# Moving casts, two weight loads and one set of transposes in the ramp of an attention + SwiGLU kernel

## The chip, the cores and the metric

One Trainium2 core of one chip. The metric is the time of one launch in device microseconds; "before" is the median of seven runs. One of these runs was profiled, and the views below are of that execution.

## The reference, cut to what matters

Sigmoid attention (8 batches, 12 heads, 448 positions, 64 per head), and a gated feed-forward block on its output:

```python
scores = q @ k.T / sqrt(64) - log(448)
x = (sigmoid(scores) @ v)              # (8, 12, 448, 64) -> (3584, 768)
g = x @ w_gate                         # 768 -> 1536
h = g * sigmoid(g) * (x @ w_val)
out = h @ w_out                        # 1536 -> 768
```

Inputs and output are float32 in DRAM.

## The kernel before, in words

**Work and names.** The attention is cut into quads: quad n is four heads of one batch, three quads a batch, 24 in all. A quad has seven chunks (n, c). `qk_tile` (L221) makes the scores of a chunk with four matmuls (L228) and `sig_tile` (L237) takes the sigmoid of 128 x 896 scores on ScalarE (L246; split in two halves at L243 for one chunk of each large visit). `pv(n)` (L249) multiplies the seven sigmoid tiles of a quad with v (28 matmuls, L260), and three VectorE copies (L269, and two at L274) bring the result into `xT`. The feed-forward block has, for each batch b, twelve units `ffn1(b, f)` (L301): six matmuls with a slice of w_gate and six with a slice of w_val (L294), then a sigmoid on ScalarE (L312) and two products on VectorE (L314, L318) into `hT`. The weights are held in four slices of three f each (wg, wv: slice i serves f = 3i to 3i+2), loaded by `w_load` (L128) on GpSimd's queue, which also turns float32 into float16 on the way. The second matrix, w_out, is used in `ffn2` (L476) and `ffn2_group` (L418) for two batches at a time.

**Making q and k ready.** For each quad, q and k are loaded (L167) as float32 into a staging tile `st`, cast to bfloat16 into `c16` (L179; on VectorE for quads 2 and 3, on GpSimd from quad 4 on) and transposed into the tile `T`. Quads 0 to 5 are transposed on TensorE (`trans_pe`, L210: fourteen matmuls with the identity, L198, into a PSUM tile, and two VectorE copies out of it, L204), the later ones by DMA (`trans_dma`, L183, on SyncE's queue). The loads of quads 0 to 3 are issued on SyncE at the start, the later ones on GpSimd, as are v (L172) and the weights. `fetch(n)` loads q, k and v of a quad, `casts(n)` casts q and k on GpSimd, `ready(n)` casts and transposes by DMA.

**What sets the order.** The order is written out by hand: each engine runs its instructions in the order of the program text, and waits at the instruction whose input or buffer isn't ready. Buffers come from pools: four `stg` staging tiles, four `c16`, five `v16`, three `T` of each kind. PSUM is one ring of four tiles of two banks each (`ring`, `Banked`, L78), taken in turn by score chunks, PVs, transposes and ffn1 units; a new user waits until the last user of its tile has been read, bank by bank where both declare their banks. A DMA issue on GpSimd's queue also waits, by its semaphore, for the eighth DMA issued before it on that queue.

**The ramp.** Lines 548 to 658 are the hand-written start: chunks of quads 0, 1 and 2, with the transposes, casts, loads and PVs of quads 0 to 2 between them, and the first three ffn1 units (`early`) begun piecewise. In the text, the casts of quad 3 stand behind those of quad 2 and ahead of pv(0).

**After the ramp.** The loop at L689 goes through the list of ffn1 and ffn2 units; between them it puts visits (`attn_step`, L535) of two to four chunks, at times that a small table of costs sets (FU1, FU2, FU3, `vtime`). The visits begin with (3,0), (3,2), (3,4), (4,0), (4,4), (5,0) and so on. A visit with a finished quad before it also does that quad's PV: (4,0) does pv(3). `plan` (L664) names what is issued after the visit that holds a given chunk: fetches, casts, transposes. `post.append` puts a quad into a list whose `trans_pe` is done right after that visit.

Of the kernel before, what the change touches and what calls it, by code (L numbers as in the profile page):

```python
# [19 lines left out]
def kernel(  # L20
# [107 lines left out]
    def w_load(kind, i):  # L128
        cs = slice(i * FW * 128, (i + 1) * FW * 128)
        if kind == "o":  # L130
            nc.gpsimd.dma_start(out=wo16[i], in_=moe_w_out[cs, :].rearrange("(f p) n -> p f n", p=128))
        else:
            w, dst = (moe_w_gate, wg16[i]) if kind == "g" else (moe_w_val, wv16[i])
            nc.gpsimd.dma_start(out=dst, in_=w[:, cs].rearrange("(j p) n -> p j n", p=128))
# [6 lines left out]
    def src_of(n, which):  # L141
        b, j = divmod(n, NJ)
        return (q, k, v)[which][b, 4 * j:4 * j + 4].rearrange("(h w) (p c) d -> (w p) h (c d)", w=2, c=C)
# [17 lines left out]
    def load(n, which, eng=None):  # L161
        ramp = 2 * n + (1 - which)
        st = (
            stg.tile([128, 2, S], FP32, tag=f"R{ramp}", bufs=1, name=f"st{which}_{n}")
            if ramp < NR else stg.tile([128, 2, S], FP32, tag="stg", name=f"st{which}_{n}")
        )
        (eng or nc.sync).dma_start(out=st, in_=src_of(n, which))  # L167
        qkv_st[(n, which)] = st

    def load_v(n):  # L170
        t = v16p.tile([128, 2, S], FP16, tag="v16", name=f"v16_{n}")
        nc.gpsimd.dma_start(out=t, in_=src_of(n, 2))  # L172
        v16[n] = t

    def cast(n, which, eng):
        st = qkv_st.pop((n, which))
        t = c16.tile([128, C, 2, D], BF16, tag="c16", name=f"c16_{which}_{n}")
        q16[(n, which, 0)] = t
        eng.tensor_copy(  # L179
            out=t.rearrange("p c h d -> p h c d"), in_=st.rearrange("p h (c d) -> p h c d", c=C)  # L180
        )
# [28 lines left out]
    def trans_pe(n):  # L210
        D2 = Banked()
        ds = [qkT.tile([128, C, 128], BF16, tag=f"T{w}", name=f"T{w}_{n}") for w in range(2)]
        for f in [trans_part(D2, w, n, w, 0, C, nc.vector, ds[w]) for w in range(2)]:
            f()
        qT[(n, 0)] = ds[0]
# [332 lines left out]
    V, G = nc.vector, nc.gpsimd  # L548
# [46 lines left out]
    def chunk(n, c):  # L595
        sig_tile(n, c, qk_tile(n, c))
# [8 lines left out]
    load_v(1)  # L605
    w_load("v", 0)
    load_v(2)
    load(4, 0, G)
    load(4, 1, G)
    load_v(3)  # L610
# [2 lines left out]
    trans_pe(1)  # L613
    cast(2, 0, V)
    cast(2, 1, V)
    cast(3, 0, V)
    cast(3, 1, V)
    chunk(0, 6)
    for c in range(3):
        chunk(1, c)  # L620
# [1 line left out]
    chunk(1, 3)  # L622
    chunk(1, 4)
    trans_pe(2)
    w_load("g", 1)
    w_load("v", 1)
    load(5, 0, G)
    load(5, 1, G)
    load_v(4)
# [26 lines left out]
    for f, Df in enumerate(early):  # L656
# [5 lines left out]

    post = []
    plan = {  # L664
        (3, 2): ((post.append, 4),),
        (3, 4): ((casts, 5),),
        (4, 0): ((fetch, 6), (post.append, 5)),
        (4, 4): ((ready, 6),),
        (5, 4): ((fetch, 7), (w_out, 0)),
        (6, 0): ((ready, 7), (w_out, 1)),  # L670
# [70 lines left out]
```

## Time and profile before

| | before |
|---|---|
| median of seven runs | 420.0 us (419.19 to 422.33) |
| the profiled execution | 420.84 us |
| its span, first to last instruction | 419.1 us |
| mean granted TensorE clock | 0.996 |
| TensorE matmul busy | 405.3 us (97%) |
| VectorE, ScalarE, GpSimd busy | 255.5, 213.9, 94.2 us |
| chain that ended last | PE 89%, DVE 3%, ACT 3%, DMA 3% |
| DMA, mean over the span | 130 GB/s; at or over 187 GB/s in the first 9 of 40 slices |

In the profile PE is TensorE (PEld its weight loads), DVE VectorE, ACT ScalarE, POOL GpSimd, SP SyncE. The 40 slices are 10.5 us each; a digit is the busy share in tenths. In a timeline a line is: start, duration, engine, line of the kernel, operation, output tile and input tiles, shapes, count of like instructions merged, and in brackets the idle time of the engine before it and what ended it. The granted clock is TensorE's, 1.00 being full speed. Matmul ends are modelled, so starts are the safer reading.

### The profile page before, as it was taken

How to read it: one execution, taken by the hardware profiler on the slowest of the kernel's cores; microseconds unless marked ns; L12 is line 12 of the kernel's file. 1: busy time of each engine (PE TensorE's matmuls, PEld its weight loads, DVE VectorE, ACT ScalarE, POOL GpSimd, SP SyncE). 2: the span in 40 equal slices, each digit the busy share in tenths (PEclk: the TensorE clock that was granted, in tenths of full speed). 3: DMA queues.
4: the chain of work that ended last, by engine and by line, in shares of the span. 5: the costliest groups of instructions: out<-in, count | busy, mean ns of one | idle time of the engine just before them, and what ended most of it. 6: DMA issues, size and time to landing. Idle time of an engine off the chain costs nothing.

```text
span 419.1 us, 7943 instructions
## 1 busy us (share of the span) xinstructions
PE 405.3 (97%) x3194; PEld 210.7 (50%) x3194; DVE 255.5 (61%) x472; ACT 213.9 (51%) x294; POOL 94.2 (22%) x125
## 2 busy tenths in 40 slices
PE   7699999999999999999999999999999999999995
PEld 3344445445555445445565445445555545555553
DVE  3726555778855546568655546568755447588653
ACT  5866787655255655655613955755715562222000
POOL 3664162355030463030030346100000000000000
PEclk9989999999999999999999999999999999999999
DMA  8999999997469987441175999430025500000135
GB/s 258 249 258 239 219 201 223 222 187 206 100 100 250 208 174 136 116 111 23 38 162 152 191 218 196 105 66 0 2 53 139 117 2 0 2 0 2 38 85 142
DMA packets 59845, 54.39 MB, mean 130 GB/s; under 512 B 35744, under 2 KB 53280, under 8 KB 59808
## 3 DMA queue, kind: packets, MB, share of 16 engines
q0 software_dynamic: 18880, 30.94, 33.6%
q1 hardware_dynamic: 40496, 22.62, 25.6%
q8 instruction: 25, 0.41, 0.4%
q10 hardware_dynamic: 432, 0.33, 0.3%
q14 instruction: 12, 0.10, 0.1%
HBM read 47.19 MB, written 11.01 MB: 139 GB/s over the span
## 4 chain that ended last, share of the span: by engine, by line
PE 89%; DVE 3%; ACT 3%; DMA 3%; issue 1%; SPq 1%; DVEq 0%; ACTq 0%
PE ps_D L294 50%; PE ps_D L418 18%; PE ps_D L228 8%; PE ps_D L260 7%; PE ps_D L476 6%; DMA st<-in_k_dram 3%; ACT pt L246 2%; DVE xT L274 1%; DVE t L314 1%; SPq L167 1%; DVE xT L269 1%; ACT s L312 1%; PE ps_D L198 1%; DVE hT L318 0%; SPq L149 0%
## 5 line engine op out<-in xcount | busy, mean ns | idle before, releaser
L246 ACT ACTIVATE pt<-ps_D,sb_t 128x896 f16<-128x896 f32 x148 | 140.6, 1012 | 83.2 <-PE ps_D L228 77.9
L294 PE MATMUL ps_D<-xT,wg 128*128 128x448 f16 x576 | 126.9, 353 | 0.9 <-DVE t L314 0.4
L294 PE MATMUL ps_D<-xT,wv 128*128 128x448 f16 x576 | 126.4, 352 | 0.0
L314 DVE TENSOR_TENSOR t<-ps_D,s 128x448 f16<-128x448 f32 x96 | 59.8, 623 | 78.3 <-ACT s L312 78.0
L312 ACT ACTIVATE s<-ps_D 128x448 f16<-128x448 f32 x96 | 52.6, 548 | 86.0 <-PE ps_D L294 74.1
L294 PEld LDWEIGHTS <-wg 128*128 128x128 f16 x576 | 53.4, 98 | 59.4 <-issue 13.8
L294 PEld LDWEIGHTS <-wv 128*128 128x128 f16 x576 | 56.3, 98 | 52.9 <-issue 0.3
L318 DVE SCALAR_TENSOR_TENSOR hT<-ps_D,t 128x448 f16<-128x448 f32 x96 | 60.0, 625 | 10.0
L179 POOL CAST c<-st 128x896 bf16<-128x896 f32 x41 | 37.9, 934 | 122.3 <-DMA T<-c 68.5
L228 PE MATMUL ps_D<-T,T 64*64 64x448 bf16 x644 | 44.6, 361 | 4.0 <-DVE xT L274 2.9
L260 PE MATMUL ps_D<-pt,v 64*64 64x448 f16 x672 | 36.6, 354 | 0.4 <-DMA v<-in_v_dram 0.4
L429 DVE TENSOR_SCALAR osb<-ps_D 128x384 f32<-128x384 f32 x43 | 24.0, 558 | 19.1 <-PE ps_D L418 18.1
L418 PEld LDWEIGHTS <-S 128*128 128x128 f16 x264 | 25.8, 98 | 17.1
L418 PE MATMUL ps_D<-wT,S 128*128 128x384 f16 x198 | 34.0, 326 | 0.0
L228 PEld LDWEIGHTS <-T 64*64 64x64 bf16 x644 | 15.3, 106 | 26.7 <-issue 21.5
L172 POOL DMA_DIRECT2D v<-in_v_dram x24 | 17.7, 737 | 42.2 <-PE ps_D L228 42.1
L260 PEld LDWEIGHTS <-v 64*64 64x64 f16 x672 | 19.7, 109 | 13.8 <-issue 1.5
L435 DVE SCALAR_TENSOR_TENSOR osb<-ps_D,osb 128x384 f32<-128x384 f32 x33 | 18.4, 558 | 13.5 <-PE ps_D L418 13.5
L274 DVE CAST xT<-ps_D 64x448 f16<-64x448 f32 x42 | 26.1, 621 | 0.7
L269 DVE CAST xT<-ps_D 128x448 f16<-128x448 f32 x24 | 15.0, 623 | 18.7 <-PE ps_D L260 13.3
L418 PEld LDWEIGHTS <-hT 128*128 128x128 f16 x198 | 18.9, 98 | 14.2 <-issue 2.1
L476 PE MATMUL ps_D<-wo,hT 128*128 128x384 f16 x144 | 24.2, 326 | 0.0
(45 smaller groups left out, 210.1 us busy)
## 6 DMA issues: line engine op xcount, KB each, us to landing
out_dram<-osb SPq DMA_DIRECT2D x52, 192.0 KB, 2.9
st<-in_q_dram POOLq DMA_DIRECT2D x20, 448.0 KB, 4.7
st<-in_k_dram POOLq DMA_DIRECT2D x20, 448.0 KB, 5.8
v<-in_v_dram POOLq DMA_DIRECT2D x24, 224.0 KB, 7.6
wg<-in_moe_w_gate_dram POOLq DMA_DIRECT2D x4, 576.0 KB, 14.8
wv<-in_moe_w_val_dram POOLq DMA_DIRECT2D x4, 576.0 KB, 14.8
wo<-in_moe_w_out_dram POOLq DMA_DIRECT2D x4, 576.0 KB, 9.9
st<-in_q_dram SPq DMA_DIRECT2D x3, 448.0 KB, 7.8
```

The lines of the kernel that those rows point to most:

```text
L179: eng.tensor_copy(out=t.rearrange("p c h d -> p h c d"), in_=st.rearrange("p h (c d) -> p h c d", c=C))
L228: nc.tensor.matmul(out=sc[w * 64:(w + 1) * 64, h2, :S], lhsT=kt[r, w * 64:(w + 1) * 64], rhs=qt[r, :, w * 64:(w + 1) * 64], start=True, st ...
L246: nc.scalar.activation(out=pt, in_=sc[:, :, :S], func=SIGM, bias=sb_t, scale=qkscale)
L260: nc.tensor.matmul(out=P[g:g + 64, h2, :S], lhsT=vt[r, h2, c * D:(c + 1) * D], rhs=pt[r, h2, :], start=(c == 0), stop=(c == C - 1),)
L274: done = [nc.vector.tensor_copy(out=o, in_=i) for o, i in halves[how:]]
L294: nc.tensor.matmul(out=D.t[:, i, :S], lhsT=w16[f // FW][:, pr, cs], rhs=xT[(b, pr)], start=(pr == 0), stop=(pr == NP - 1),),
L312: D.read(nc.scalar.activation(out=s16, in_=D.t[:, 0, :S], func=SIGM), 0)
L314: D.read(nc.vector.tensor_tensor(out=t1, in0=D.t[:, 0, :S], in1=s16, op=MULT), 0)
L318: nc.vector.scalar_tensor_tensor(out=hT[(b // 2, f)][:, b % 2, :], in0=D.t[:, 1, :S], scalar=HSC, in1=t1, op0=MULT, op1=MULT),
L418: nc.tensor.matmul(out=D.t[:, bank, :hw], lhsT=l, rhs=B_(i), start=(first and i == 0), stop=(i == HF - 1), skip_group_check=True,),
L429: nc.vector.tensor_scalar(out=o, in0=D.t[:, bank, :hw], scalar1=HREC, scalar2=None, op0=MULT), bank
L476: nc.tensor.matmul(out=D.t[:, half, :hw], lhsT=h[:, m * 128:(m + 1) * 128], rhs=wo16[f // FW][:, f % FW, half * hw:(half + 1) * hw], start ...
```

## The change

Three edits, all of order. No instruction is added or taken away, and SyncE's queue is the same.

1. The two casts of quad 3 (VectorE) go from behind the casts of quad 2 to behind `trans_pe(2)`, so that on VectorE the copies of pv(0) and of the quad 2 transposes come ahead of them.
2. The loads of the second slices of w_gate and w_val go from behind `trans_pe(2)` to ahead of the loads of quad 4; on GpSimd's queue they move past q4, k4 and v3.
3. In `plan`, the casts of quad 5 go from the visit (3,4) to the visit (3,2), and the TensorE transposes of quad 5 from behind the visit (4,0), which does pv(3), to behind the visit (3,4), which does no PV. On GpSimd's queue the casts of quad 5 keep their place among its instructions.

```diff
@@ -605,6 +605,8 @@
     load_v(1)
     w_load("v", 0)
     load_v(2)
+    w_load("g", 1)
+    w_load("v", 1)
     load(4, 0, G)
     load(4, 1, G)
     load_v(3)
@@ -613,8 +615,6 @@
     trans_pe(1)
     cast(2, 0, V)
     cast(2, 1, V)
-    cast(3, 0, V)
-    cast(3, 1, V)
     chunk(0, 6)
     for c in range(3):
         chunk(1, c)
@@ -622,8 +622,8 @@
     chunk(1, 3)
     chunk(1, 4)
     trans_pe(2)
-    w_load("g", 1)
-    w_load("v", 1)
+    cast(3, 0, V)
+    cast(3, 1, V)
     load(5, 0, G)
     load(5, 1, G)
     load_v(4)
@@ -662,9 +662,9 @@
 
     post = []
     plan = {
-        (3, 2): ((post.append, 4),),
-        (3, 4): ((casts, 5),),
-        (4, 0): ((fetch, 6), (post.append, 5)),
+        (3, 2): ((casts, 5), (post.append, 4)),
+        (3, 4): ((post.append, 5),),
+        (4, 0): ((fetch, 6),),
         (4, 4): ((ready, 6),),
         (5, 4): ((fetch, 7), (w_out, 0)),
         (6, 0): ((ready, 7), (w_out, 1)),
```

## Prediction

> **What bounds the kernel now.** I read the page first (busy shares, then the 40 slices), then the idle time of each engine in order of time, then the chain of waits, then tables of short stretches for the granted clock, and last single DMA issues with their landings. The span is 419.1 us; the same execution took 420.84 us, so 1.74 us lie around the span, and it is 0.84 above the median of 420.0. All sums below start from 420.84.
>
> ```profile
> PE   7699999999999999999999999999999999999995
> ...
> PEclk9989999999999999999999999999999999999999
> ```
>
> TensorE is at 90% or more in all slices from the third (21 us) on; its busy time is 405.3 of 419.1 us. So an edit pays only where TensorE stands still, and that is in the first 60 us. TensorE's timeline shows it (start, duration, engine and line, work, and in brackets the idle time before it and what ended it):
>
> ```profile
> 16.06 0.94 PE L198 MATMUL ps_D<-idn,c 128*128 128x128 bf16 x14 [0.51 <-ACT pt L246]
> 19.14 0.57 PE L228 MATMUL ps_D<-T,T 64*64 64x448 bf16 x8 [2.14 <-DVE xT L274]
> ...
> 26.26 0.38 PE L228 MATMUL ps_D<-T,T 64*64 64x448 bf16 x4 [0.79 <-DVE xT L274]
> ...
> 48.87 0.57 PE L228 MATMUL ps_D<-T,T 64*64 64x448 bf16 x8
> ...
> 50.73 1.29 PE L294 MATMUL ps_D<-xT,wg 128*128 128x448 f16 x6 [0.40 <-DVE xT L274]
> ```
>
> The longest stop inside the program is the 2.14 us before 19.14: chunk(1,5) needs the PSUM tile of pv(0) back, and VectorE has not copied it. VectorE's timeline says why:
>
> ```profile
> 14.31 0.85 DVE L179 CAST c<-st 128x896 bf16<-128x896 f32 x1 [0.60 <-DMA st<-in_q_dram]
> 16.64 0.63 DVE L179 CAST c<-st 128x896 bf16<-128x896 f32 x1 [1.48 <-DMA st<-in_k_dram]
> 17.18 0.62 DVE L269 CAST xT<-ps_D 128x448 f16<-128x448 f32 x1
> 17.83 1.25 DVE L274 CAST xT<-ps_D 64x448 f16<-64x448 f32 x2
> ```
>
> The two casts of quad 3 wait 0.60 and 1.48 us for loads (k3 lands at 16.6), and the copies of pv(0), whose last matmul ended at 15.0, stand behind them in VectorE's queue until 17.2. ScalarE, which paces this ramp with one 0.9 us sigmoid after the other, loses 1.76 us there:
>
> ```profile
> 19.57 6.88 ACT L246 ACTIVATE pt<-ps_D,sb_t 128x896 f16<-128x896 f32 x7 [1.76 <-PE ps_D L228]
> 26.74 1.01 ACT L246 ACTIVATE pt<-ps_D,sb_t 128x896 f16<-128x896 f32 x1 [0.29 <-ACT pt L246]
> 27.93 1.01 ACT L246 ACTIVATE pt<-ps_D,sb_t 128x896 f16<-128x896 f32 x1 [0.18 <-PE ps_D L228]
> ```
>
> The stop has an after-effect. In this table of stretches the first columns are length and TensorE's busy time; the third from the right is its granted clock:
>
> ```profile
> 6.38:9.79 3.41, 2.12 (x30) 1.00 (x30) 1.25 (x4) 2.87 (x4) 1.37 (x2) 1.00 1.03 389
> ...
> 16.62:20.04 3.42, 1.28 (x22) 0.85 (x20) 3.32 (x6) 1.66 (x3) 0.82 (x1) 1.00 1.30 204
> 20.04:23.45 3.41, 3.41 (x39) 2.09 (x39) 1.49 (x3) 3.27 (x5) 1.25 (x2) 0.50 1.22 295
> ```
>
> After a stretch with 37% busy the clock is 0.50 for the next 3.4 us; after one with 62% (6.38 to 9.79) it stayed at 1.00. So pv(1), 28 matmuls from 22.05, is issued in 2.0 us where the chain shows 1.3 elsewhere.
>
> **Part 1, casts of quad 3 behind pv(0)'s copies and the transposes of quad 2.** Nothing is added; two casts of 0.63 move past three copies of xT and two of T, 0.62 to 0.63 each. Walked instruction by instruction, with durations from the rows above:
> - VectorE: xT copies 15.05 to 16.95 (3 x 0.63); the quad 2 transposes on TensorE still run from 16.06 to 17.0; copies of T2 17.0 to 18.15; casts of quad 3 18.1 to 19.25 (k3 is there since 16.6, so they no longer wait).
> - TensorE: chunk(1,5) at 17.0 for 19.14, chunk(1,6) behind it. What is late next: the transposes of quad 3 stand before chunk(2,0) in TensorE's order and now wait for the moved casts; q's at 18.7, k's at 19.3, chunk(2,0) at 19.65. Gap 17.6 to 18.7 instead of 17.0 to 19.1. T3's copies end at 20.55, pv(1) starts then, ends at 22.05, its xT copies at 24.0, so chunk(2,5), which waits for them, comes at 24.05 for 26.26.
> - ScalarE: (1,5) straight after (1,4) at 17.6, (2,0) at 20.1 for 21.6, then 0.9 apart, (2,6) at 25.65 for 27.93.
> - pv(2) starts at 27.05; before, at 29.37. **Gain 2.3 us**, and from 29.37 on TensorE stood still for only 0.09 us until 48, so the gain lasts if nothing else becomes late.
>
> This assumes clock 1.00. TensorE would be busy for about 2.2 of the 3.42 us from 16.62 to 20.04 (0.38 of the quad 2 transposes, 0.6 of two chunks, 1.1 of the quad 3 transposes, rest of chunk(2,0)), 64%: nearest to the row that kept its clock (62%), far from 37%. If it does fall at 20.0, the chunks (0.375 each) and pv(1) (7 x 0.375) run until 23.5, the copies until 25.5, and the gain is 0.8. Both ends stay: 0.8 to 2.4.
>
> On this clock the Trainium skill (TensorE: Matmul & The Clock Gate, section Why this matters for your kernels) says to avoid idle gaps over about 3 us, since one idle window brings the slow clock back. Here 2.14 us idle, with 0.5 just before it, was enough, so the measured rows decide; by the rule no gap of the changed kernel could lower the clock, which gives the same sum as mine.
>
> **Part 2, the second FFN1 slices ahead of quad 4.** On GpSimd's queue wg1 and wv1 (L134) move past q4, k4 and v3. A single issue's row gives its time to landing:
>
> ```profile
> 14.68 0.90 POOL L134 DMA_DIRECT2D wg<-in_moe_w_gate_dram x1
> 18.66 0.82 POOL L134 DMA_DIRECT2D wv<-in_moe_w_val_dram x1 [3.09 <-DMA v<-in_v_dram]
> ...
> 25.82 1.81 POOL L179 CAST c<-st 128x896 bf16<-128x896 f32 x2
> 27.57 0.82 POOL L134 DMA_DIRECT2D wv<-in_moe_w_val_dram x1
> ```
>
> wg1 took 15.0 and wv1 14.7, so they land at 29.7 and 33.4. The landings come in order of issue: v2 23.5, q4 24.7, k4 25.9, v3 26.8, wg1 29.7, wv1 33.4, q5 34.5, k5 35.7, v4 36.7, wg2 39.6, wv2 42.5; a weight slice adds 2.9, a q, k or v 1.0 to 1.2. With the new order: wg1 26.4, wv1 29.3, q4 30.5, k4 31.6, v3 32.6, and the rest as before or 0.8 earlier (wv1's step was 3.7 before). By itself this gains nothing: f=3 (gate at 34.86, value at 36.0) waited for neither. But part 1 brings its value matmuls to 33.7, 0.3 after the old landing of wv1; the new order makes that 4.4, so it protects part 1.
> Its price is on GpSimd: casts(4) wait for k4 and end at 32.6 instead of 27.6, and wv2, v5, wg3, wv3, casts(5), load 6 stand behind them. The transposes of quad 4 come at 38.3 (40.61 less 2.3): 5.7 to spare. wv2 is issued at 32.6 for 27.57. The queue in front of it still holds v3 to wg2, until 38.8, so I take its landing as 41.7 to 42.5, against its use at 44.2 (f=6, 45.60 less 2.3 plus 0.95 of part 3). Casts(5) end at 37.6, load 6 is issued at 37.6 to 39.8 (36.7 before) and lands behind wv3 as before, at about 50.6. SP's queue is not changed.
>
> A rule that speaks against this is in the Trainium skill (DMA: Bandwidth & Descriptors, section Queues, rings and completion order): transfers of one queue may finish out of order. The landings listed do come in order; if the rule bit here, wv2 could come late, which is the third rival.
>
> **Part 3, transposes of quad 5 behind the visit (3,4) without a PV.** Fourteen transposes and two copies move; none is added. Before, pv(3) and these transposes took neighbouring PSUM tiles, and VectorE had five copies to make between two units: chunk(4,2) came at 48.87 where pv(3), from 47.23 with 1.32 for its 28 matmuls, was out at 48.55 (0.3 lost, to VectorE's hT of f=6), and f=7 waited 0.40 for the copies of pv(3). Both go: at the new place (44.46) the transposes take the tile of f=5, whose products end at 44.0 and 44.7 bank by bank; f=6 then takes the tile of chunk(3,4), whose sigmoid ends at 45.2, before the transposes end at 45.4; f=7 gets the tile of chunk(4,1), not of pv(3). Casts(5) end at 37.6, needed at 42.2. What is late next is f=8 behind f=7's product by some 0.2. **Gain 0.7**, ends 0 (the wait passes to f=8) and 0.85.
>
> Sum: 420.84 - 2.3 - 0.7 = **417.8 us**. Against the median of 420.0 that is 2.2, or 0.5%; about 0.3%, 1.26 us, is what a measurement of this kernel can tell from no change. Ends: 420.84 - 2.4 - 0.85 = 417.6, and 420.84 - 0.8 = 420.0.
>
> **Rivals.**
> 1. The clock falls all the same (in another execution the slow stretch may start elsewhere): 420.84 - 0.8 - 0.7 = 419.3. For it: the gap of 1.1 us that stays and 0.5 before it. Against it: 64% busy.
> 2. The gain is given back, the transfer being the bound anyway: DMA ran without pause until 52 us and its times do not move, while TensorE comes 3.0 earlier. The DMA transpose of k6 (issued at 53.10, 7.1 to landing, 60.2) is used at 66.42, now 63.4: 3.2 to spare. If load 6, 0.9 later in issue, and the transposes queued behind load 7 cost more than that, up to 3 us go: 417.8 to 420.8, taken as 420.6.
> 3. Slower: wv2 late. Its issue moves to 32.6; if its own 14.9 to landing, or wg3's 16.5, counts from there, it lands at 47.5 to 49.1, and f=6 waits 3.3 to 4.9 from 44.2: 421.1 to 422.7, taken as 421.9. It decides from a landing after 44.2; slower than this execution from 47.2. Against it: those 14.9 were queueing, and the queue is shorter by the 5 us.
>
> **How the numbers follow.** Forecast 0.66, rival 1 0.12, rival 2 0.12, rival 3 0.10. Faster by over 0.3% (below 418.74): the forecast and a little of rival 1, 0.67. Slower (above 421.26): rival 3 for the most part, 0.09. Within: 0.24. The range goes from 416.9 (0.7 under the best end, for execution noise: the seven runs differ by more than that) to 420.2, past rival 1 and the low end of part 1, and leaves most of rivals 2 and 3 out.
>
> **What would show it.** Right: VectorE's xT copy near 15.1; chunk(1,5) near 17; clock 1.00 throughout from 16 to 30; pv(2) near 27; wv1 landing near 29 and wv2 near 42; no idle of TensorE before f=7. Wrong: clock 0.50 anywhere after 16 us (rival 1); a TensorE wait for a T or c tile at 60 to 70 us (rival 2); TensorE waiting on wv before f=6 (rival 3).

## The result, and the profile after

The changed kernel takes 417.86 us (median of 20 runs, 417.22 to 418.88) against 420.0 before (median of 47 runs, 419.1 to 422.33); ratio 0.9945, interval 0.9933 to 0.9956. Its profiled execution took 417.39 us with a span of 415.6, against 420.84 and 419.1. One of the twelve runs of the changed kernel in e5 (below) took 701.49 us at a mean granted clock of 0.558; the ratios, intervals and counts below leave it out.

TensorE's timeline after the change, over the places where it stood still before:

```profile
15.88 0.94 PE L198 MATMUL ps_D<-idn,c 128*128 128x128 bf16 x14 [0.52 <-ACT pt L246]
16.81 0.57 PE L228 MATMUL ps_D<-T,T 64*64 64x448 bf16 x8
18.53 1.10 PE L198 MATMUL ps_D<-idn,c 128*128 128x128 bf16 x14 [1.15 <-ACT pt L246]
...
20.41 1.52 PE L260 MATMUL ps_D<-pt,v 64*64 64x448 f16 x28
...
27.05 1.52 PE L260 MATMUL ps_D<-pt,v 64*64 64x448 f16 x28
...
47.03 0.55 PE L228 MATMUL ps_D<-T,T 64*64 64x448 bf16 x8
47.51 1.31 PE L294 MATMUL ps_D<-xT,wg 128*128 128x448 f16 x6
...
49.88 0.76 PE L228 MATMUL ps_D<-T,T 64*64 64x448 bf16 x12
50.73 1.29 PE L294 MATMUL ps_D<-xT,wg 128*128 128x448 f16 x6
```

Chunks (1,5) and (1,6) follow the quad 2 transposes at once (16.81); the stop of 2.14 us is now one of 1.15 before the quad 3 transposes; pv(2) starts at 27.05 for 29.37; f=7 (47.51) has no wait in front of it. VectorE shows the first cause, and ScalarE what is left of its 1.76 us:

```profile
14.84 0.62 DVE L269 CAST xT<-ps_D 128x448 f16<-128x448 f32 x1 [0.75 <-PE ps_D L260]
15.50 1.26 DVE L274 CAST xT<-ps_D 64x448 f16<-64x448 f32 x2
16.79 1.15 DVE L204 COPY T<-ps_D 128x896 bf16<-128x896 bf16 x2
17.86 1.15 DVE L179 CAST c<-st 128x896 bf16<-128x896 f32 x2
```

```profile
20.05 6.58 ACT L246 ACTIVATE pt<-ps_D,sb_t 128x896 f16<-128x896 f32 x7 [0.63 <-ACT pt L246]
```

The casts (17.86) wait for nothing and end at 19.01; the page names a sigmoid as what ended the 1.15 us before 18.53, but that sigmoid had ended at 17.62 and the first cast at 18.48: it is the cast. In the table of stretches (third column from the right: granted clock) the two around the old stop are 67% and 79% busy, and the clock stays:

```profile
14.51:17.92 3.41, 2.29 (x38) 1.28 (x26) 3.00 (x6) 3.41 (x5) 1.43 (x2) 1.00 1.28 210
17.92:21.33 3.41, 2.71 (x46) 1.87 (x50) 2.25 (x5) 2.78 (x4) 1.45 (x2) 1.00 1.31 204
```

GpSimd's queue shows the price of the weight order: wg2 waits for wg1's landing and wv2 stands behind the casts of quad 4, at 33.16 for 27.57.

```profile
27.03 0.84 POOL L134 DMA_DIRECT2D wg<-in_moe_w_gate_dram x1 [2.26 <-DMA wg<-in_moe_w_gate_dram]
...
33.16 0.82 POOL L134 DMA_DIRECT2D wv<-in_moe_w_val_dram x1
```

Issue by issue: wv1 16.0 us from 13.6 to landing (29.6), wv2 9.1 from 33.2 (42.3, before 42.5): 5.6 us later in issue, and no later in landing.

### The profile page after: what moved, and what is told of

It reads as the page before. It is cut to its first block, busy times and chain, and to the rows that moved or that the text cites. A ratio compares the mean times of both kernels' runs of the same rounds, so it can differ in the third digit from the quotient of the medians.

```text
span 415.6 us, 7945 instructions
## 1 busy us (share of the span) xinstructions
PE 403.3 (97%) x3194; PEld 209.9 (51%) x3194; DVE 256.6 (62%) x472; ACT 213.6 (51%) x294; POOL 94.3 (23%) x125
## 4 chain that ended last, share of the span: by engine, by line
PE 90%; ACT 3%; DMA 3%; DVE 2%; issue 1%; SPq 0%; POOL 0%; DVEq 0%; ACTq 0%
PE ps_D L294 51%; PE ps_D L418 18%; PE ps_D L228 7%; PE ps_D L260 7%; PE ps_D L476 6%; ACT pt L246 2%; DMA v<-in_v_dram 2%; DMA st<-in_q_dram 1%; DVE t L314 1%; PE ps_D L198 1%; ACT s L312 1%; DVE xT L269 0%; ACT pt L243 0%; DVE xT L274 0%; DVE T L204 0%
```

## The experiments

Each group of runs was timed beside before on the same chip (its median there in brackets). "pv(0) to pv(2)" is the time between the starts of these two on TensorE, which takes out that the ramp itself starts up to 0.4 us earlier or later in an execution. In e7 and e8 pv(0) itself ran at clock 0.50, so their figures can't be compared with the others.

| run | median us (before) | ratio, 95% interval | pv(0) to pv(2) |
|---|---|---|---|
| before, profiled | | | 15.92 |
| after, profiled | | | 13.85 |
| e1 part 1 alone | 418.87 (420.33) | 0.9979, 0.9964 to 0.9994 | 13.84 |
| e2 part 2 alone | 419.71 (420.33) | 0.9992, 0.9978 to 1.0006 | 16.19 |
| e3 part 3 alone | 418.58 (420.33) | 0.9959, 0.9944 to 0.9975 | 15.06 |
| e4 parts 1 and 3 | 417.72 (420.33) | 0.9946, 0.9930 to 0.9961 | 14.08 |
| e5 after | 418.08 (419.64) | 0.9965, 0.9952 to 0.9979 | 13.85 |
| e6 before, filled | 420.01 (419.64) | 1.0011, 0.9991 to 1.0031 | 14.35 |
| e7 casts on GpSimd | 417.10 (419.64) | 0.9945, 0.9925 to 0.9965 | 14.08 |
| e8 wv2 later | 419.98 (419.64) | 1.0007, 0.9991 to 1.0024 | 15.16 |
| e9 after | 417.58 (420.80) | 0.9940, 0.9919 to 0.9961 | 13.87 |
| e10 casts on GpSimd | 417.38 (420.80) | 0.9935, 0.9914 to 0.9956 | 13.12 |
| e11 the same, no part 2 | 417.08 (420.80) | 0.9933, 0.9907 to 0.9959 | 13.12 |

### The three parts alone (e1 to e4)

e1 has the first edit of the diff, e2 the second, e3 the third, e4 the first and the third.

> Part 1 alone (casts of quad 3 moved; weights and quad 5 as before). My theory: this edit carries most of the change. In a profile, xT copies of pv(0) near 15, pv(2) near 27.05 for 29.37, clock 1.00 from 16 to 30; wv1 lands at 33.4 where the value matmuls of f=3 now want it at 33.7, so part 2 is worth 0 to 0.2 here. Time: the whole change gave 2.1 by medians, part 3 takes 0.7 to 0.9 of it, so 418.6 to 418.8 (0.9970). Rival (the earlier weight slices carry it): f=3 waits for wg1 or wv1, pv(2) earlier but f=4 not, time near 420.0.

> Part 2 alone (wg1, wv1 ahead of quad 4). My theory: no TensorE wait of before is for a weight, so 420.0 within 0.3%; in a profile wg1 lands near 26.5 and wv1 near 29.5, wv2 near 42, no new TensorE wait. Rival (weights carry the change): faster by over 1 us. Rival (late wv2): issued near 33, lands near 48, f=6 waits 2 us or more, slower.

> Part 3 alone (transposes of quad 5 behind the visit without a PV). My theory: the 0.3 before chunk(4,2) and the 0.40 before f=7 go: 0.7 to 0.9 off, 419.1 to 419.3 (0.998). Rival (the wait passes to f=8): f=8 waits 0.5 or more for the products of f=7, time 420.0.

> Parts 1 and 3 without part 2. My theory: part 2 only keeps a margin: wv1 lands at 33.4, wanted at 33.7, so 417.9 as with all three, or up to 0.3 more. Rival (part 2 is needed): f=3 waits for wv1 by 0.5 or more, 418.4 or more.

e1: as expected in the ramp (pv(2) at 27.22), and the two waits of part 3 are still there, 0.32 us before chunk(4,2) (46.73, where pv(3) from 45.09 was out after 1.32) and 0.40 before f=7:

```profile
46.73 0.57 PE L228 MATMUL ps_D<-T,T 64*64 64x448 bf16 x8 [0.15 <-DVE hT L318]
...
48.59 1.29 PE L294 MATMUL ps_D<-xT,wg 128*128 128x448 f16 x6 [0.40 <-DVE xT L274]
```

In time e1 gave a little less than expected (0.9979 for 0.9970, which its interval still holds) and e3 more (0.9959 for 0.998): the medians do not bear out that part 1 carries most of the change.

e2: no gain that its interval can tell; wv1 landed at 30.0, wv2 was issued at 33.4 and landed at 42.5. Both rivals fall. Its profile repeats the stop and the clock of before:

```profile
16.48:19.89 3.41, 1.02 (x19) 0.66 (x16) 2.85 (x5) 1.40 (x2) 0.29 (x1) 1.00 1.30 204
19.89:23.30 3.41, 3.41 (x38) 2.32 (x38) 1.96 (x4) 2.93 (x4) 1.16 (x2) 0.50 1.30 203
```

e3: faster than I expected (418.58 for 419.1 to 419.3). From pv(2) to the start of f=7 it takes 20.45 us, before 21.36: 0.91 for part 3. At f=8, 0.73 of it is left (23.68 against 24.41), since f=8 starts 0.16 late. The rest of this profile's lead is the clock: the stop was there, 2.34 us long, but it fell on two stretches, 52% and 57% busy, and the clock stayed:

```profile
4.43:7.84 3.41, 2.12 (x23) 1.03 (x22) 1.69 (x5) 1.83 (x4) 1.28 (x2) 1.00 0.91 294
7.84:11.26 3.42, 3.08 (x28) 1.73 (x29) 1.66 (x3) 3.26 (x4) 2.67 (x4) 0.50 1.08 340
14.67:18.08 3.41, 1.78 (x30) 1.25 (x23) 1.80 (x4) 3.10 (x4) 0.97 (x2) 1.00 1.28 214
18.08:21.50 3.42, 1.96 (x30) 1.25 (x30) 3.33 (x6) 1.76 (x2) 1.53 (x2) 1.00 1.31 205
```

```profile
16.80 0.63 DVE L179 CAST c<-st 128x896 bf16<-128x896 f32 x1 [1.58 <-DMA st<-in_k_dram]
```

That splits part 1, by pv(0) to pv(2): 15.92 with stop and slow clock, 15.06 with the stop alone (e3), 13.84 with neither (e1). But k3 lands at its own time in each execution (its cast starts 3.19 after pv(0) before, 3.33 in e3). From that cast to pv(2), which leaves this out, it is 12.73 with the slow clock (16.64 to 29.37) and 11.73 without (16.80 to 28.53); e2 (12.67) and e6 below (11.72) repeat both. So about 1.0 of the 2.1 us is the clock and 1.1 VectorE's queue.

e4: as fast as the whole change; wv1 landed at 32.6 and its matmuls ran at 34.19 without a wait. Part 2 is worth nothing that these runs can tell.

At like clock the parts add up. A whole stretch of 3.41 us at 0.50 takes 0.004 off the mean clock of a run, so a run with a mean of 0.997 or more holds none. The medians of such runs in this group: before 419.54 (8 of 23 runs), e1 418.69 (6 of 12), e2 418.91 (3 of 12), e3 418.53 (3 of 6), e4 417.57 (4 of 6). That is 0.85, 0.6, 1.0 and 2.0 less than before. These are few runs, and the 0.6 of e2 leaves a small gain of part 2 open.

### The clock alone (e5, e6)

The edit of e6, against before (the helpers that take the number of repeats are left out):

```diff
-    trans_pe(2)
+    trans_pe(2, 3)        # each transpose three times, into the same place
```

> The changed kernel once more, as the other side of the comparisons of this group. 417.8, as measured; a mean granted clock of 0.997 or more in nearly all runs, where before often has 0.996 and less.

> Before, with each transpose of quad 2 done three times into the same PSUM place: 28 more matmuls of 128 columns, about 1.6 us of TensorE work inside the 2.1 us stop, with VectorE's order as before. It asks what the granted clock alone costs. My theory: TensorE's busy share around the stop goes from 37% to over 70%, the clock stays at 1.00 behind it, chunk(1,5) still comes at 19.1 to 19.3, and pv(2) at 28.4 to 28.6 for 29.4: 0.85 of the 2.3 us. Time 419.2 to 419.5 by medians. Rival (the stop alone counts, the clock is hidden by ScalarE): pv(2) near 29.4, 420.0. Rival (the clock is all): pv(2) near 27.1, 418.0.

The expectation of e5 missed on the clock: 7 of its 12 runs have a mean of 0.997 or more, not nearly all.

```profile
15.90 2.50 PE L198 MATMUL ps_D<-idn,c 128*128 128x128 bf16 x42 [0.40 <-ACT pt L246]
18.74 0.57 PE L228 MATMUL ps_D<-T,T 64*64 64x448 bf16 x8 [0.33 <-DVE xT L274]
```

```profile
16.24 0.63 DVE L179 CAST c<-st 128x896 bf16<-128x896 f32 x1 [1.18 <-DMA st<-in_k_dram]
```

In this profile of e6 the mechanism is as expected: TensorE is filled, the clock stays at 1.00, and chunk(1,5) still waits for VectorE (18.74). Pv(0) to pv(2) takes 14.35, less than expected, since k3 came 0.56 earlier after pv(0)'s start than in the profile of before (cast at 16.24, 2.63 after pv(0)). But the time missed: 420.01 for 419.2 to 419.5, no faster than before. The granted clock of the single runs explains it only in part. It is 0.997 or more in 8 of the 12 runs, and in 12 of 29 of before, so the slow stretch is rarer but not gone; in profiles of other kernels it lies elsewhere in the ramp (from 7.84 in e3, 13.03 in e7, 12.27 in e8), where this filling doesn't reach. But at like clock, too, e6 is no faster: 419.70 in those 8 runs, against 419.36 in the 12 of before. In its profile, the 1.41 us by which pv(2) is earlier than before are 1.12 at the last matmul. Why the time doesn't fall stays open; the 1.0 us of the clock is shown in the ramp of single profiles, not in the time.

### What is late next (e7, e9, e10, e11)

The casts of quad 3 go to GpSimd, against the changed kernel (shortened at the dots; the removed lines stood behind `trans_pe(2)`); e11 also takes part 2 back.

```diff
     load(4, 1, G)
+    cast(3, 0, G)
+    cast(3, 1, G)
     load_v(3)
...
-    cast(3, 0, V)
-    cast(3, 1, V)
```

> The changed kernel, with the casts of quad 3 on GpSimd between the issues of k4 and v3, where GpSimd stood idle from 15.9 to 19.0, in place of VectorE. It asks whether what is late next is, as I said, the wait of the quad 3 transposes for those casts. My theory: casts end at 17.8 for 19.0, the transposes come at 17.7 to 17.9 for 18.5, ScalarE goes on without its gap of 0.6, chunk(2,0) at 18.5 for 19.6; pv(1) then waits for v1 (19.8), so pv(2) comes 0.5 to 0.7 earlier: 417.2 to 417.4. Rival (ScalarE is the bound already): pv(2) and time as in the changed kernel. Rival (v3 or q5 later in GpSimd's queue): a TensorE wait for a transfer near f=3 to f=6, slower.

> The changed kernel as the other side of this group: 417.8 to 418.1.

> The casts of quad 3 on GpSimd once more, since the profile of the first try had a slow stretch of the clock at 13.0 us and pv(0) at half speed, so that it could not show the step. My theory, where the clock stays at 1.00: the quad 3 transposes near 17.8, ScalarE without the gap of 0.63 before chunk(2,0), pv(2) near 26.4 for 27.05, time 0.6 to 1.0 under the changed kernel of this group. Rival (the first result was luck of the clock): within 0.3 of it.

> The same, but with the second weight slices where before has them (part 2 undone). It asks what the weight order is worth once TensorE comes earlier still. My theory: the value matmuls of f=3 come near 33.0 and wv1 lands at 32.5 to 33.7, so a wait of 0 to 0.7, and a time 0 to 0.7 over the run with part 2. Rival (part 2 has no value at any speed): the same time, no wait.

The profile of e7 ran pv(0) at half speed (from 13.85, 2.77 us for 28 matmuls), after a stretch 54% busy:

```profile
9.61:13.03 3.42, 1.85 (x30) 1.21 (x30) 2.53 (x4) 3.42 (x5) 3.42 (x5) 1.00 1.12 319
13.03:16.44 3.41, 3.41 (x37) 1.83 (x40) 0.63 (x1) 3.41 (x4) 3.41 (x5) 0.50 1.25 248
```

e10 shows the step clean, on TensorE and on ScalarE:

```profile
18.03 0.94 PE L198 MATMUL ps_D<-idn,c 128*128 128x128 bf16 x14 [0.32 <-ACT pt L246]
...
26.66 1.52 PE L260 MATMUL ps_D<-pt,v 64*64 64x448 f16 x28
```

```profile
12.46 13.77 ACT L246 ACTIVATE pt<-ps_D,sb_t 128x896 f16<-128x896 f32 x15
```

Fifteen sigmoids run without a gap: the wait for the moved casts was what came late next, worth 0.75 us in the ramp (13.87 to 13.12), and now ScalarE is the pace of the ramp. In time, e10 missed: it is 0.20 under the changed kernel of its group, for 0.6 to 1.0 expected, and within the 0.3 of its rival. e7 is 0.98 under its own and e11 0.50; the intervals overlap. So that the version with GpSimd casts beats before is shown, that it beats the changed kernel is likely and not shown by time. The profile of e10 shows where the step went: pv(2) comes 0.52 earlier than in e9 (26.66 for 27.18), but later, in ffn2, TensorE waits 0.45 for VectorE where it does not in e9, and at the last matmul a lead of 0.06 is left.

```profile
103.82 7.96 PE L476 MATMUL ps_D<-wo,hT 128*128 128x384 f16 x48 [0.45 <-DVE osb L489]
```

e11 is the one for part 2's value: wv1 landed at 32.7, and f=3 did not wait though its value matmuls came at 33.13:

```profile
33.13 1.30 PE L294 MATMUL ps_D<-xT,wv 128*128 128x448 f16 x6
```

The margin is down to 0.4 us there; the rival (part 2 has no value at any speed tried) holds.

### Place in the queue (e8)

```diff
-    w_load("v", 2)
     load_v(5)
     w_load("g", 3)
+    w_load("v", 2)
     w_load("v", 3)
```

> The changed kernel, with the third slice of w_val issued behind v5 and the fourth slice of w_gate in place of ahead of them; its issue is some 1.5 us later. It asks whether landings go by place in the queue. My theory: by place it lands 1.1 + 2.9 later, near 46.3, and the value matmuls of f=6, which want it at 44.1, wait 2.1: near 419.9. Rival (issue time counts): it lands near 43.7, no wait, 417.8; or, with 14.9 us from the issue, near 49.6, a wait of 5.5, 423.

```profile
44.40 1.29 PE L294 MATMUL ps_D<-xT,wg 128*128 128x448 f16 x6
46.67 1.31 PE L294 MATMUL ps_D<-xT,wv 128*128 128x448 f16 x6 [0.97 <-DMA wv<-in_moe_w_val_dram]
```

Issued at 35.0, wv2 took 11.6 to its landing at 46.6, where place in the queue put it (46.3); counted from the issue, 43.7 or 49.6 were expected. In this profile the ramp was 1.5 later than in the changed kernel's, so f=6 lost 1.1 (45.54 to 46.67) for 2.1. By medians it is 1.9 slower than the changed kernel of its group.

## Why the prediction was right

**Part 1.** The walk held step by step: xT copies 14.84 (15.05 forecast), chunk(1,5) 16.81 (17.0), quad 3 transposes 18.53 (18.7), pv(1) 20.41 (20.55), pv(2) 27.05 (27.05). The busy share that it put at 64% from 16.62 to 20.04 measured 66% (2.27 us), though the terms it lists for it add up to 2.5 us, not 2.2. That pv(2) came at 27.05 to the hundredth is luck: the ramp began 0.25 earlier (v0 landed at 13.2 for 13.4), and by pv(0) to pv(2) the gain is 2.07, not 2.3.

What the sum did not say is that about 1.0 of it is a slow clock that before does not always have there. Of the 71 runs of before in the three groups, 28 have a mean clock of 0.997 or more and a median of 419.36, the other 43 one of 420.74; of 41 runs of the changed kernel 28 have 0.997 or more (417.72), 13 less (418.45). At like clock the change gives 1.6 us (1.5 and 1.8 within the groups of e5 and e9); where it gives more, it also has the slow stretch less often. A low mean does not say where the slow time lies: in the profile after the change the clock is at 0.50 from 413.9 us to the end, behind the last matmul, where it costs nothing. The three profiles of the changed kernel (after, e5, e9) have no slow stretch in the ramp, those of e7 and e8 have one before part 1's place. So rival 1 is no other outcome: it can have happened in up to a third of the runs, and these take 0.7 longer, for 1.5 forecast.

**Part 2.** The landings came as forecast, 0.3 to 0.6 late (wg1 26.8, wv1 29.6, v3 33.2), and wv2 (42.3) within its bounds. That it gains nothing by itself agrees with e2. That it protects part 1 was not seen: none of the profiles with part 1 and without part 2 waited for wv1. It landed at 33.7 in e1, 0.2 before its matmuls (33.85), and 1.6 and 0.4 before them in e4 and e11 (32.6 and 32.7). So the margin it adds is there, and these executions did not need it.

**Part 3.** The mechanism was right, and the term came out at its size because two errors cancel. Up to f=7 it measured 0.9, not 0.7 (pv(2) to f=7: 21.36 before, 20.46 after). I took the 0.40 us of idle in front of f=7 as the loss; but idle counts from the modelled end of the last matmul. By starts, the transposes from 49.38 at 0.056 each let the next matmul go at 50.17, and it went at 50.73: 0.56, and with the 0.32 before chunk(4,2) it is 0.88. And f=8 gives some back: it starts 0.85 after the three chunks ahead of it (49.88 to 50.73), which take 0.69 elsewhere, so 0.16 are lost, where the forecast named 0.2 and did not take it off. At the start of f=8 part 3 has 0.73 left (pv(2) to f=8: 24.41 before, 23.68 after).

**The sum.** From profile to profile the time fell by 3.45 for 3.0: 2.3 in the ramp, 0.7 in part 3, 0.1 later, and 0.33 behind the last matmul (5.11 to 4.78 us from its start to the end of the span), which no term of the forecast holds. The three profiles with neither part 2 nor part 3 (before, e1, e6) have 5.10 to 5.11 there, the ten others 4.74 to 4.79; why is open. That the median, 417.86, lies within 0.1 of the forecast is in part luck: the profiled execution is 0.4 below it, and the runs with a lower clock pull the median up again.

**Rivals 2 and 3.** The DMA transpose of k6 landed at 61.1, its use came at 63.21: no wait, 2.1 us in hand. wv2 kept its place in the queue. The Trainium skill's rule (DMA: Bandwidth & Descriptors, Queues, rings and completion order), that transfers of one queue may finish out of order, is written there of the queues of SyncE and ScalarE. On GpSimd's queue it did not show in any landing read here (in the profile after the change wg1 26.8, wv1 29.6, v3 33.2, wg2 39.3, wv2 42.3, in the order of issue), and e8 moved the landing by the queue's place.

## What to carry to other kernels

An instruction that waits for a transfer should not stand in an engine's queue ahead of one that frees a buffer: here 1.5 us of waiting for k3 held back copies that were ready. Read a loss from start to start, and ask what comes late next: the same two casts, moved to an idle engine, gave another 0.75 us in the ramp, of which a later wait took 0.45 back in one profile (e10). The landing of wv2 in its full queue followed its place there, not its issue: issued 5.6 us later it landed no later, and two places further back it landed 4.3 us later (e8). And compare runs of like clock: before's own runs are 1.4 us apart by it.

## What the runs showed of the hardware

The granted clock falls in whole stretches of 3.41 us that lie on a fixed grid within one execution, at another phase in the next (in e7 it rises at 16.44 and falls again at 415.80, 117 times 3.413 us later, behind the last matmul); the Trainium skill (TensorE: Matmul & The Clock Gate, Part 1: The HAM clock gate) describes such a free-running window of 3413 ns, and the tables agree. After a stretch with 30% or 37% of TensorE busy the next was at 0.50 (e2, before). Between 52% and 62% both outcomes occur: 54% in e7, 59% in e8 and 62% in e3 lost the clock, 52% and 57% in e3 and 62% before did not. What decides there is open. The same page's advice (Why this matters for your kernels) to avoid idle gaps over about 3 us does not cover this: gaps of 2.14 and 2.39 us were enough when one stretch held them whole, 2.34 us across two (e3) were not, and in the stretches of e3, e7 and e8 that lost the clock no gap was longer than 0.6.
